# Pairs of batches swept as a wave in a fixed table of issue; value product and keys/values products in eight 64x32 fp32 tiles of TensorE, weights unsplit

## The chip, the cores and the metric

The kernel runs on one core of a Trainium2 chip. The metric is the time that the device takes for one run of the program, in microseconds (us). Lower is better. The kernel before took 899.54, 896.29 and 899.51 us in three runs, a median of 899.51 us. For this kernel, differences under about half a per cent cannot be told from none.

## The reference

An attention over a small memory, then a gated feed-forward block. Batch 8, 8 heads, 576 positions, head size 64, 32 memory slots; 4608 tokens of width 512, and 1536 hidden columns.

```python
a = phi - np.max(phi, axis=2, keepdims=True)
a = np.exp(a)
a = a / (np.sum(a, axis=2, keepdims=True) + 1e-09)
k_m = np.einsum('bhsm,bhsd->bhmd', a, k)
v_m = np.einsum('bhsm,bhsd->bhmd', a, v)
scores = scale * np.matmul(q, k_m.transpose(0, 1, 3, 2))
scores = scores - np.max(scores, axis=-1, keepdims=True)
attn = np.exp(scores)
attn = attn / (np.sum(attn, axis=-1, keepdims=True) + 1e-09)
x = (attn @ v_m), heads side by side      # 4608 x 512
xn = x / np.sqrt(np.mean(x * x, axis=-1, keepdims=True) + 1e-06) * rms_g
g = xn @ w_gate                           # 512 -> 1536
out = (silu(g) * (xn @ w_val)) @ w_out    # 1536 -> 512
```

All inputs and the output are float32. Products on TensorE are either fp32 (each matmul is then two instructions in the profile, a first and a second pass over the weights) or "fp32r" in three terms: an operand is split into a high part and a rest, and high times high, high times low and low times high are added.

## The kernel before, in words

**Pairs and columns.** The eight batches form four pairs. The attention of a token is a row of 32 numbers per head, so `attn @ (v_m @ W)` replaces `(attn @ v_m) @ W`: for each pair and each block of hidden columns, the **value product** (`vw_steps`, L824) multiplies the pair's memory values by the gate and value weights, and the gate and value products (`gv_steps`, L872) multiply the result by the attention rows. There are 12 blocks of 128 hidden columns and 4 pairs, so 48 steps, numbered i in the names (`vp17`, `hf17`).

**Phase 1.** For every batch: the maximum of phi (`prep`, L485: `mc` L493, `mt`, `mx`, `mb`, `mr`), the subtraction (L526), the exponential (L536), the keys/values product `kvp` (`kv_steps`, L556; matmuls at L567 in 128x64 tiles, in which the exponentials `e_bd` are laid out as two heads with zero blocks between them, and sums at L582), and a transpose of the result. Pairs 0 and 1 are attended here: queries are turned (`qtp`, L679), scores `S` L700, maximum and subtraction L711 and L713, exponential L720, sums and norm L727 to L740, then transposes of the attention rows (`tp`, L189, copied at L199), the product that gives each token's square (`xp` L240, L253), its root by Newton steps (L264 to L281), and the scaling and splitting of the attention rows (`rp` L209, `at` L217, `ath` L228, `atl` L229).

**Sweeps.** Pairs 0 and 1 go through the 12 column blocks first, then pairs 2 and 3. A step i is: the value product, 12 fp32r matmuls of 256 columns (L843), split by ACT and DVE into `xh` (L867) and `xl` (L868); four gate and four value products of 6 matmuls, 256 or 320 columns wide (L890), with silu on ACT (`sg` L898) and the multiplication on DVE (`hf` L899); the split of the hidden rows into `hh` on ACT (L912) and `hl` on POOL (L913). Every second i, the output product `po` (L932): 54 matmuls of 512 columns over two blocks, added into `acc` on ACT (L937) or DVE (L939). Pairs 2 and 3 are attended by `attend_steps` (L959) in the first sweep.

**Weights.** They come as 64-bit numbers; `convert` (L340) makes them float32 with bit operations (abs L349, clamp L350, shift L359, add L366, join L379), and splits all of them into a high and a low part (`wh`, `oh` L396 on ACT; `wl`, `ol` L397 on POOL). The split parts are written to memory and read back for the second sweep (`reload`, L410).

**What sets the order.** Each step is entered into a list with a due time from a table of numbers (`PRM`); the sorted list is the program, and the tool that builds it then orders the instructions by its own estimate. The order is fixed when the program is built. Each engine, and SP's queue of transfers, works through its own list in that order; it waits where an operand or a buffer is not ready.

Of the kernel before, what the change touches and what calls it, by code (L numbers as in the profile page):

```python
# [19 lines left out]
XTTR = True  # L20

# [3 lines left out]
WB = 3  # L25
PRM = dict(
    K_AT=[12.08, 15.05, 41.68, 67.52, 100.72, 122.69, 147.6, 167.28],
    KP=0.82,
    POST=[-0.15, 3.05, 3.9, 7.72, 15.27, 21.96],
    P1=4.13,  # L30
    PREP=[-1.56, 0.79, 2.32, 3.9, 18.7],
    PD=[2.1, 11.67, 7.79, 18.42, 7.54, 2.17],
    EXP=[1.89, 13.89, 3.07, 6.96, 11.93, 1.72],
    ES=1.16,
    PH=[9.86, 15.89, 41.23, 73.43, 103.91, 132.92],
    S_AT=[32.67, 47.44, 51.02, 69.42, 103.56, 112.2, 119.41, 123.39],
# [12 lines left out]
    CV2=155.67,
    CP2=0.05,  # L50
    QE=[0, 0],
    CE=[2, 1],
    XE=[28, 29, 14, 13],
    ESN=[3, 3, 2, 3, 3, 3, 2, 3],
    SUM=[1, 0, 1, 0, 2, 1, 2, 1],
    CA=1,
    B=[2, 2, 2],
    RO=3.35,
    RS=4.63,
    RP=2.84,  # L60
    GV=[0.12, 0.256, 0.267, 0.683, 0.84, 0.979],
    VW=[-0.204, 0.03, 0.165],
    VW0=0.296,
    O=[0.115, 0.297, 0.451, 0.524, 0.954, 0.957, 1.344, 1.487, 1.518],
    PRE=[-0.525, 1.142, 1.893, 2.147, 2.545, 2.788],
    PI=0.0157,
    PSW=[1.728, 2.047, 2.009, 2.653, 2.96, 3.24],
    SU=[1.874, 3.014, 5.716, 6.6, 9.746, 12.208, 13.357, 15.533],
    AO=[0.162, 0.169, 0.192, 0.276, 0.385, 0.474, 0.562, 0.581, 0.59, 0.601, 0.728, 0.804, 1.158, 1.217],
    XB=[17.199, 22.916],  # L70
    XS=[0.1086, 0.0359],
    XM=[21.887, 24.858],
    XN=[0.012, 0.176, 0.184, 0.33, 0.33, 0.566, 0.596, 0.699, 0.766],
    LV=[22.571, 24.198],
    CB=1,
)


def weave(*lists):

    order = []
    for li, entry in enumerate(lists):
        steps, lo, hi = entry if isinstance(entry, tuple) else (entry, 0.0, 1.0)
        n = len(steps)
        for i, s in enumerate(steps):
            order.append((lo + (hi - lo) * (i + 0.5) / n, li, i, s))
    order.sort(key=lambda e: e[:3])  # L90
    for e in order:
        e[3]()
# [3 lines left out]
def kernel(  # L96
# [12 lines left out]

    nc = tc.nc
    P = 128
# [9 lines left out]
    G = 2  # L133
# [7 lines left out]
    vm = {}  # L141
    gram = {}
    gb = persist.tile([P, 2, 2, P], F32, name="gb")
    dram = ctx.enter_context(tc.tile_pool(name="dram", bufs=1, space=bass.MemoryType.DRAM))
    gram_dram = {i: dram.tile([P, 2, 2, 64], F32, name=f"gd{i}") for i in range(G, NP)}
    a_dram = {i: dram.tile([P, NT, 256], F32, name=f"ad{i}") for i in range(G, NP)}
    rinv = [persist.tile([P, NT], F32, name=f"rinv{i}") for i in range(NP)]
    at_hi, at_lo = {}, {}

    vg_dram = {b: dram.tile([P, HP, 64], F32, name=f"vgd{b}") for b in range(2 * G, B)}  # L150
    km_late = {b: persist.tile([P, HP, 64], F32, name=f"km{b}") for b in range(2 * G, B)}
    ssqs = {}
    w_dram = {j: dram.tile([P, 2, HP, 2, P], F32, name=f"wd{j}") for j in range(NJ)}
    o_dram = {j: dram.tile([P, 2, 512], F32, name=f"od{j}") for j in range(NJ)}

    def new_vm(pr):
        vm[pr] = persist.tile([P, 2, 2, 2, 2, 64], F32R, tag=f"vm{pr % G}", name=f"vm{pr}")

    def split_v(b, vg):
        pr, j = divmod(b, 2)  # L160
        for e in range(2):
            o = e ^ j
            src = vg.rearrange("p (c e) m -> p c e m", e=2)[:, :, o, :]
            hi, lo = vm[pr][:, 0, :, e, o, :], vm[pr][:, 1, :, e, o, :]
            nc.scalar.copy(hi, src)
            nc.gpsimd.tensor_tensor(out=lo, in0=src, in1=hi.bitcast(F32), op=ALU.subtract)

    def x_steps(pr, a, psum_t, psum_x, fetch=None):

        tps, xps, srcs, st = {}, {}, {}, {}  # L170
        i = pr % G

        def first():
            st["at"] = persist.tile([P, NT, 2, P], F32, tag="at", name=f"at{pr}")
            ssqs[pr] = persist.tile([P, NT], F32, tag=f"ssq{i}", name=f"ssq{pr}")
            for par in range(2):
                rows = slice(64 * par, 64 * par + 64)
                (nc.scalar.copy if pr < G else nc.sync.dma_start)(gb[rows, :, :, rows], gram[pr][rows])

        def turn(t0):  # L180
            n = min(2, NT - t0)

            def f():
                tps[t0] = tp = psum_t(f"tp{pr}_{t0}")
                for t in range(t0, t0 + n):
                    srcs[t] = src = a(t)
                    for cc in (1, 0):
                        o = 2 * (t - t0) + cc
                        nc.tensor.transpose(  # L189
                            out=tp[:, o * P:(o + 1) * P], in_=src[:, cc * P:(cc + 1) * P],  # L190
                            identity=ident,
                        )
            return f

        def copy(t0):
            n = min(2, NT - t0)

            def f():
                (nc.scalar.copy if PRM["XE"][pr] & (1 << t0 // 2) else nc.vector.tensor_copy)(  # L199
                    st["at"][:, t0:t0 + n].rearrange("p t c x -> p (t c x)"), tps.pop(t0)[:, :256 * n]  # L200
                )
            return f

        def spread(t0, n):

            def f():
                tps["r", t0] = tp = psum_t(f"rp{pr}_{t0}")
# [6 lines left out]
            def g():  # L214
                at = st["at"][:, t0:t0 + n]
                tp = tps.pop(("r", t0))[:, :n * P].rearrange("p (t x) -> p t x", x=P)
                nc.vector.tensor_tensor(  # L217
# [902 lines left out]
```

## Time and profile before

| | before |
|---|---|
| runs | 899.54, 896.29, 899.51 us (median 899.51) |
| the profiled execution's own time | 896.89 us |
| its span in the trace | 895.1 us |
| PE busy | 835.6 us (93%), 6207 matmul instructions |
| DVE busy | 559.0 us (62%) |
| ACT busy | 422.0 us (47%) |
| POOL busy | 286.7 us (32%) |

The profile divides the span by engine and by source line. A matmul's duration in it is its passage through a pipeline, longer than the distance to the next one: what a stream of matmuls costs is read from the start times. In the names, the number of the buffer is left out; the arrow points from inputs to output.

### The profile page before, as it was taken

The numbers are of one execution on the slowest core, as the hardware profiler recorded it, in microseconds if no ns is written. First come the engines' busy times: TensorE is split into PE (matmuls) and PEld (weight loads), VectorE is DVE, ScalarE is ACT, GpSimd is POOL, SyncE is SP. The second block draws the span as 40 slices with busy tenths as digits, with TensorE's granted clock in tenths as the row PEclk, the third lists the DMA queues.
The fourth block names the chain that finished last, engine by engine and source line by source line (L and its number), as shares of the span: only waits on it lengthen the run. The fifth ranks groups of instructions, "written<-read, shape, count | busy, mean of one in ns | idle before, by whom it ended". The sixth has DMA issues, their size and how long they took to land.

```text
span 895.1 us, 15791 instructions
## 1 busy us (share of the span) xinstructions
PE 835.6 (93%) x6207; PEld 741.3 (83%) x6207; DVE 559.0 (62%) x956; ACT 422.0 (47%) x719; POOL 286.7 (32%) x242
## 2 busy tenths in 40 slices
PE   4989586999998999999999999899999999999997
PEld 4777476899987988897788997898889999999996
DVE  5577958985778868878845746622545555455543
ACT  2666435787765645656532532344333323333330
POOL 3463735533524414323422421511211112211120
PEclk9899788999999999999999999999999999999999
DMA  8987553652644422534222143502204012040046
GB/s 292 320 263 239 204 169 101 223 168 60 217 114 153 150 61 95 163 105 142 102 73 93 60 117 102 135 1 72 70 4 139 1 63 79 1 142 1 9 110 141
DMA packets 81506, 106.41 MB, mean 119 GB/s; under 512 B 34324, under 2 KB 52248, under 8 KB 81432
## 3 DMA queue, kind: packets, MB, share of 16 engines
q1 hardware_dynamic: 81432, 105.41, 38.0%
q8 instruction: 49, 0.80, 0.4%
q14 instruction: 25, 0.20, 0.1%
HBM read 73.93 MB, written 31.46 MB: 118 GB/s over the span
## 4 chain that ended last, share of the span: by engine, by line
PE 74%; DVE 10%; issue 5%; DMA 5%; ACT 4%; POOL 1%; SPq 1%; DVEq 0%; POOLq 0%; ACTq 0%
PE po L932 29%; PE pv L890 15%; PE pg L890 14%; PE vp L843 6%; PE kvp L567 3%; DMA phi<-in_phi_dram 2%; PE xp L240 2%; DVE w L379 2%; DVE xl L868 1%; DVE ex L350 1%; DMA raw<-in_moe_w_out_dram 1%; PE qtp L679 1%; PE S L700 1%; DVE acc L939 1%; DVE mc L493 1%
## 5 line engine op out<-in xcount | busy, mean ns | idle before, releaser
L913 POOL TENSOR_TENSOR hl<-hf,hh 128x512 fp32r<-128x512 f32 (+1 forms) x96 | 141.4, 1474 | 405.9 <-ACT hh L912 392.3
L939 DVE TENSOR_TENSOR acc<-po,acc 128x512 f32<-128x512 f32 x180 | 123.1, 687 | 128.2 <-PE po L932 127.6
L932 PE MATMUL po<-oh,hh 128*128 128x512 f32 x432 | 172.4, 400 | 3.0 <-DVE acc L939 2.0
L932 PE MATMUL po<-oh,hl 128*128 128x512 f32 x432 | 170.6, 395 | 0.0
L932 PE MATMUL po<-ol,hh 128*128 128x512 f32 x432 | 170.4, 394 | 0.0
L898 ACT ACTIVATE sg<-pg 128x256 f32<-128x256 f32 x192 | 78.1, 411 | 163.2 <-PE pg L890 151.6
L868 DVE TENSOR_TENSOR xl<-vp,xh 64x1024 fp32r<-64x1024 f32 x94 | 114.7, 1220 | 52.3 <-ACT xh L867 51.2
L899 DVE TENSOR_TENSOR hf<-pv,sg 128x256 f32<-128x256 f32 x192 | 85.2, 452 | 71.6 <-PE pv L890 49.0
L867 ACT CAST xh<-vp 64x1024 fp32r<-64x1024 f32 x94 | 94.8, 1008 | 49.7 <-PE vp L843 23.9
L912 ACT CAST hh<-hf 128x512 fp32r<-128x512 f32 (+1 forms) x96 | 64.7, 674 | 81.9 <-DVE hf L899 59.5
L932 PEld LDWEIGHTS po<-oh,hl 128*128 128x128 f32 x432 | 81.2, 188 | 19.3
L932 PEld LDWEIGHTS po<-oh,hh 128*128 128x128 f32 x432 | 81.1, 188 | 17.0 <-DVE acc L939 2.9
L890 PE MATMUL pg<-ath,xh 128*128 128x320 f32 (+1 forms) x384 | 87.3, 300 | 5.7 <-ACT sg L898 3.0
L932 PEld LDWEIGHTS po<-ol,hh 128*128 128x128 f32 x432 | 81.3, 188 | 11.0
L843 PE MATMUL vp<-wh,vm 128*128 128x256 f32 x384 | 85.4, 286 | 3.6 <-DVE xl L868 2.8
L890 PE MATMUL pv<-ath,xh 128*128 128x320 f32 (+1 forms) x384 | 85.0, 299 | 1.1 <-DVE hf L899 0.9
L890 PE MATMUL pg<-atl,xh 128*128 128x320 f32 (+1 forms) x384 | 84.9, 297 | 0.0
L890 PE MATMUL pg<-ath,xl 128*128 128x320 f32 (+1 forms) x384 | 84.7, 295 | 0.0
L890 PE MATMUL pv<-atl,xh 128*128 128x320 f32 (+1 forms) x384 | 84.5, 296 | 0.0
L890 PE MATMUL pv<-ath,xl 128*128 128x320 f32 (+1 forms) x384 | 83.2, 296 | 0.0
L890 PEld LDWEIGHTS pg<-ath,xh 128*128 128x128 f32 x384 | 63.5, 189 | 12.0 <-ACT sg L898 4.8
L843 PEld LDWEIGHTS vp<-wh,vm 128*128 128x128 f32 x384 | 65.4, 189 | 6.7 <-DVE xl L868 2.3
(129 smaller groups left out, 1338.3 us busy)
## 6 DMA issues: line engine op xcount, KB each, us to landing
kv<-in_k_dram SPq DMA_DIRECT2D x32, 288.0 KB, 5.2
kv<-in_v_dram SPq DMA_DIRECT2D x32, 288.0 KB, 5.8
out_dram<-acc SPq DMA_DIRECT2D x72, 128.0 KB, 2.4
raw<-in_moe_w_gate_dram SPq DMA_DIRECT2D x12, 512.0 KB, 5.0
raw<-in_moe_w_val_dram SPq DMA_DIRECT2D x12, 512.0 KB, 3.9
wd<-wh SPq DMA_DIRECT2D x12, 512.0 KB, 3.4
wd<-wl SPq DMA_DIRECT2D x12, 512.0 KB, 4.2
raw<-in_moe_w_out_dram SPq DMA_DIRECT2D x12, 512.0 KB, 4.2
```

Of the source, the lines that this page charges most:

```text
L240: nc.tensor.matmul(xp[64 * j:64 * j + 64, P * cc:P * cc + P], st["at"][:, t, cc, 64 * j:64 * j + 64], gb[:, j, cc], start=True, stop=True,)
L567: nc.tensor.matmul(kvp[64 * par:64 * par + 64, cc, 0:128], e_bd[j][:, hp, c, :], st["kv", b, hp][:, :, 64 * c:64 * c + 64], start=(c == 0) ...
L843: nc.tensor.matmul(vp[:, e, :], lhs(l), r[:, 2 * cc + e, :], start=(n == 0), stop=(n == 2),)
L867: nc.scalar.copy(xh[rows], src)
L868: nc.vector.tensor_tensor(out=xl[rows], in0=src, in1=xh[rows].bitcast(F32), op=ALU.subtract)
L890: nc.tensor.matmul(pt[:, :N], l[:, cc, b, half * P:half * P + P], r[:, b, cc, t0:t0 + n, :].rearrange("p t x -> p (t x)"), start=(m == 0), ...
L898: nc.scalar.activation(sg[:, :N], pg[:, :N], AF.Silu)
L899: nc.vector.tensor_tensor(out=hf[:, :, b, :], in0=pv[:, :N].rearrange("p (t x) -> p t x", x=64), in1=sg[:, :N].rearrange("p (t x) -> p t x ...
L912: nc.scalar.copy(hh, hv)
L913: nc.gpsimd.tensor_tensor(out=hl, in0=hv, in1=hh.bitcast(F32), op=ALU.subtract)
L932: nc.tensor.matmul(po, l[:, tt, :], r, start=(m == 0), stop=(m == 5))
L939: nc.vector.tensor_tensor(out=accs[key], in0=po, in1=accs[key], op=ALU.add)
```

## The change

1. **Wave.** The two sweeps become one list of 24 pairs of blocks, `ORDER`, in which pair 0 starts alone, pair 1 joins after four double blocks, and pairs 2 and 3 follow one after the other. Only pair 0 is attended ahead of the sweep; the products of batches 2 to 7 and the attention of pairs 1 to 3 are issued among the sweep's steps.
2. **Table of issue.** All steps are cut into single instructions or small groups (2933 in all), and a table `ISSUE` gives the place of each; `perform` issues them in that order, and the builder's own ordering is switched off.
3. **Value product.** 16 fp32 matmuls of 64 rows by 32 columns of weights and 256 moving columns (L1002) in place of 12 fp32r matmuls of 128x128. The gate and value weights stay unsplit (`wc`), and so do the memory values (`vm`); what is stored and read back halves. `xh` and `xl` are made in two instructions of 128x512 (L1020, L1018) in place of two of 64x1024.
4. **Keys/values product.** 64x32 tiles without the zero blocks, 72 matmuls per batch (L436) in place of 36 in 128x64 tiles.
5. **Smaller edits.** The weights' last step (join) goes from DVE to POOL (L948); Newton's steps go from four to three, and the root is done in two parts (`fin`); the sums of the attention rows are all on DVE.

```diff
@@ (value product)
-                for e in range(2):
-                    def lhs(vt):
-                        return vt[:, cc, e].rearrange("p o x -> p (o x)")
-                    for n, (l, r) in enumerate(((vh, wh), (vh, wl), (vl, wh))):
-                        nc.tensor.matmul(
-                            vp[:, e, :], lhs(l), r[:, 2 * cc + e, :],
-                            start=(n == 0), stop=(n == 2),
-                        )
+            for cc in range(2):
+                for b in range(2):
+                    for g in range(4):
+                        hp, h = 2 * cc + g // 2, g % 2 ^ flip(b, cc)
+                        rows = slice(64 * h, 64 * h + 64)
+                        nc.tensor.matmul(
+                            vp[32 * g:32 * g + 32, flip(b, cc), cc, :],
+                            vm[pr][rows, b, hp, 32 * (g % 2):32 * (g % 2) + 32],
+                            w[rows, hp, :],
+                            start=True, stop=True,
+                        )
@@ (keys/values product)
+                for c in range(c0, c1):
+                    for cc, hp, rows, to in tiles():
+                        nc.tensor.matmul(
+                            st["kvp", b][cc][to, 0:128],
+                            e_of(b)[rows, hp, c, :],
+                            st["kv", b, hp][rows, :, 64 * c:64 * c + 64],
+                            start=(c == 0), stop=(c == NT - 1),
+                        )
@@ (order of the blocks)
+ORDER = [
+    (0, 0), (0, 1), (0, 2), (0, 3), (1, 0), (0, 4), (1, 1), (0, 5), (1, 2), (1, 3), (1, 4), (1, 5), (2, 0), (2, 1), (2, 2), (2, 3), (2, 4), (2, 5), (3, 0), (3, 1), (3, 2), (3, 3), (3, 4), (3, 5),
+]
```

`flip(b, cc)` is `(b + cc) % 2`. For one half of the batch (cc, b) the four matmuls use both row halves and all four column groups, and all four write the same bank of PSUM; each b takes the row halves the other way round, so the two b together name all eight tiles.

**Where instructions stand now.** On PE late in the sweep. Before, `vp33` is the value product of step 33, `wh17` and `wl17` its split weights, `pv31` and `pg31` a value and a gate product of step 31, `po29` an output product:

```order
L932 MATMUL po29_5_7238<-ol15_7108,hh29_1_7093 128x512
L932 MATMUL po29_5_7238<-oh15_7107,hl29_1_7094 128x512
L890 MATMUL pv31_10_7331<-ath3_6446,xh31_7137 128x320 x2
L890 MATMUL pv31_10_7331<-atl3_6447,xh31_7137 128x320 x2
L890 MATMUL pv31_10_7331<-ath3_6446,xl31_7138 128x320 x2
L843 MATMUL vp33_7347<-wh17_7246,vm2_5874 128x256
L843 MATMUL vp33_7347<-wl17_7247,vm2_5874 128x256
L843 MATMUL vp33_7347<-wh17_7246,vm2_5874 128x256 x2
L843 MATMUL vp33_7347<-wl17_7247,vm2_5874 128x256
L843 MATMUL vp33_7347<-wh17_7246,vm2_5874 128x256
L890 MATMUL pg31_11_7354<-ath3_6446,xh31_7137 128x320 x2
L890 MATMUL pg31_11_7354<-atl3_6447,xh31_7137 128x320 x2
```

After, at the corresponding kind of place (`vp40` is the value product of step 40, `wc40` its unsplit weights):

```order
L1095 MATMUL po37_0_8870<-oh37_8694,hh37_0_8713 128x512
L1095 MATMUL po37_0_8870<-ol37_8695,hh37_0_8713 128x512
L1095 MATMUL po37_0_8870<-oh37_8694,hl37_0_8715 128x512
L1002 MATMUL vp40_8879<-wc40_7763,vm3_6254 32x256 x16
L1095 MATMUL po37_2_8901<-oh36_8835,hh36_0_8603 128x512
L1095 MATMUL po37_2_8901<-ol36_8836,hh36_0_8603 128x512
L1095 MATMUL po37_2_8901<-oh36_8835,hl36_0_8606 128x512
```

All sixteen stand together, between two groups of 128x128 matmuls. Before, the rows show six of the twelve, of the same tile size as their neighbours; the other six stand further on.

On PE before the first gate product, the products of all eight batches, here the last one, stood ahead of it (`kvp7`, and `rp1`, the second pair's scaling):

```order
L582 MATMUL kvp7_1617<-ones_118,es7_1546 64x1 x2
L582 MATMUL kvp7_1617<-ones_118,e_bd1_132 64x1
L582 MATMUL kvp7_1617<-ones_118,es7_1546 64x1 x2
L582 MATMUL kvp7_1617<-ones_118,e_bd1_132 64x1
L209 MATMUL rp1_0_1752<-ident_58,rinv1_71 128x128 x4
L209 MATMUL rp1_4_1762<-ident_58,rinv1_71 128x128 x4
L611 MATMUL kvt7_1747<-ident_58,kb7_1743 128x128 x2
L611 MATMUL kvt7_1747<-ident_58,vb7_1744 128x128 x2
L209 MATMUL rp1_8_1768<-ident_58,rinv1_71 128x128
L636 MATMUL kvt7_1747<-vt7_1758 64x64 x4
L843 MATMUL vp0_0_1804<-wh0_1361,vm0_456 128x256
```

After (`vp2`, the third value product; `mr3`, the maximum of the fourth batch; `pv0` and `pg0`, value and gate products; `kvp3`, the fourth batch's keys/values product):

```order
L1002 MATMUL vp2_1141<-wc2_1002,vm0_469 32x256 x16
L378 MATMUL mr3_0_1165<-ident_72,mb3_0_1058 128x128
L1038 MATMUL pv0_10_1170<-ath0_1103,xh0_847 128x320 x2
L1038 MATMUL pv0_10_1170<-atl0_1108,xh0_847 128x320 x2
L1038 MATMUL pv0_10_1170<-ath0_1103,xl0_882 128x320 x2
L1038 MATMUL pg0_00_1188<-ath0_1103,xh0_847 128x256 x2
L1038 MATMUL pg0_00_1188<-atl0_1108,xh0_847 128x256 x2
L1038 MATMUL pg0_00_1188<-ath0_1103,xl0_882 128x256 x2
L1038 MATMUL pv0_00_1195<-ath0_1103,xh0_847 128x256 x2
L1038 MATMUL pv0_00_1195<-atl0_1108,xh0_847 128x256 x2
L1038 MATMUL pv0_00_1195<-ath0_1103,xl0_882 128x256 x2
L436 MATMUL kvp3_0_1208<-kv3_0_1011,e_bd1_126 32x128 x2
```

Batches 3 to 7 have moved behind the first gate and value products.

On DVE around the first multiplication of gate and value (`hf0`): weights (`ex2`, `w2`) and the split of the value products (`xl0`, `xl1`) stood ahead of it, and all of phase 1 before them:

```order
L858 TENSOR_TENSOR xl0_1819<-vp0_0_1804,xh0_1818 64x512 x2
L858 TENSOR_TENSOR xl0_1819<-vp0_1_1811,xh0_1818 64x512 x2
L350 TENSOR_SCALAR ex2_1_1967<-ex2_1_1967 128x512
L359 TENSOR_SCALAR ex2_1_1967<-ex2_1_1967 128x512
L366 SCALAR_TENSOR_TENSOR ex2_1_1967<-raw_21_1733,ex2_1_1967 128x512
L379 ISA w2_1_1982<-mi2_1_1970,ex2_1_1967 128x1024
L868 TENSOR_TENSOR xl1_1892<-vp1_1839,xh1_1891 64x1024
L899 TENSOR_TENSOR hf0_0_1846<-pv0_00_1848,sg0_00_1861 128x4x64
```

After (`at0` is the first pair's scaling, `wex` the weights, `phi3` the fourth batch's subtraction):

```order
L1018 TENSOR_TENSOR xl1_1117<-vp1_1039,xh1_1060 128x512
L767 TENSOR_TENSOR at0_679<-at0_679,rp0_8_1126 128x256
L934 SCALAR_TENSOR_TENSOR wex1_3_1086<-raw_13_1005,wex1_3_1086 128x512
L387 TENSOR_TENSOR phi3_754<-phi3_754,mr3_0_1165 128x1152
L915 TENSOR_SCALAR wex2_1_1182<-wex2_1_1182 128x512
L927 TENSOR_SCALAR wex2_1_1182<-wex2_1_1182 128x512
L934 SCALAR_TENSOR_TENSOR wex2_1_1182<-raw_21_1084,wex2_1_1182 128x512
L1054 TENSOR_TENSOR hf0_0_1205<-pv0_00_1195,sg0_00_1203 128x4x64
L1054 TENSOR_TENSOR hf0_1_1244<-pv0_10_1170,sg0_10_1241 128x5x64
```

What comes ahead of the first `hf` is now one pair's attention, batches 0 to 2 and the start of batch 3; batches 3 to 7 and three pairs' attention follow it.

More of the change, by code (lines that the diff above doesn't have):

```diff
@@ L95, with flat, perform @@
+ON_SCALAR = (21, 28, 14, 13)
+ISSUE = [
[159 rows of a table added]
+]
+def flat(f):
+    return [h for g in f for h in flat(g)] if isinstance(f, list) else [f]
+def perform(tc, parts):
+    assert sorted(ISSUE) == list(range(len(parts)))
+    with tc.manual_schedule():
+        for n in ISSUE:
+            parts[n]()
 @with_exitstack
@@ L168, in x_steps @@
[L168 to L176, printed above, removed]
+    at_hi, at_lo, vm, gram, ssqs = {}, {}, {}, {}, {}
+    ones = sl.tile([P, 1], F32, name="ones")
+    V.memset(ones, 1.0)
+    hmask = sl.tile([P, 3], F32, name="hmask")
@@ new lines, with flip, bank @@
+    for g in range(4):
+        for c in range(3):
+            V.memset(hmask[32 * g:32 * g + 32, c:c + 1], float((g + c) % 2 == 0))
+    rg = sl.tile([P, HP], F32, name="rg")
+    def flip(b, cc):
+        return (b + cc) % 2
+    e_bd = {}
+    e_bd[0] = persist.tile([P, 2, HP, NT, M], F32, tag="ath1", name="e_bd0")
+    e_bd[1] = persist.tile([P, 2, HP, NT, M], F32, tag="atl1", name="e_bd1")
+    nc.gpsimd.memset(gb, 0.0)
+    def bank(tag, name, shape=None):
+        return ps.tile(shape or [P, 512], F32, tag=tag, name=name)
@@ new lines, with load_rg, put_rg, small @@
+    for t in ("vw",):
+        ps.tile([P, 2, 2, 256], F32, tag="vw", name="vw_first", bufs=1)
+    for t in "gvo":
+        bank(t, f"{t}_first")
+    load = nc.sync.dma_start
+    st = {}
+    def load_rg():
+        rows = st["rg_rows"]
+        st["rg_ps"] = tp = bank("o", "rg_ps")
+        nc.tensor.transpose(out=tp[:, :HP], in_=rows, identity=ident[:HP, :HP])
+    def put_rg():
+        V.tensor_copy(rg, st["rg_ps"][:, :HP])
+    def small(b):
+        return sa if b < 2 else sl
+    def load_phi(b):
+        if b < 2:
+            t = sa.tile([P, HP, NT, M], F32, tag="phi", name=f"phi{b}")
+        else:
+            t = sl.tile([P, HP, NT, M], F32, tag="phi", name=f"phi{b}")
+        n = 2 if b == 0 else HP
+        for i in range(0, HP, n):
+            load(
+                t[:, i:i + n].rearrange("p hp c m -> p hp (c m)"),
+                phi[b].rearrange("(hp h) (p c) m -> (h p) hp (c m)", h=2, c=NT)[:, i:i + n],
+            )
+        st["phi", b] = t
@@ new lines, in f, with add @@
+            return [mm, add] + ([put] if u == NU - 1 else [])
+        return [f(t) for t in range(NT)]
+    parts = []
+    def add(*steps):
+        parts.extend(flat(list(steps)))
+    load_phi(0)
+    st["rg_rows"] = sa.tile([HP, P], F32, name="rg_rows", bufs=1)
+    load(st["rg_rows"], rms_g.rearrange("(hp r) -> hp r", r=P))
+    for hp in range(HP):
+        load_kv(0, hp)
+    load_phi(1)
+    for hp in range(HP):
+        load_kv(1, hp)
+    add(prep(0, 0, 2), prep(0, 2, 4)[:-1], prep(1))
@@ L1080 @@
-    for a, p in enumerate(PRM["SU"]):
-        ev += place(p, PRM["AO"], attend_steps(G + a // HP, a % HP))
-    for a in range(NP - G):
-        steps = x2(G + a)
-        n = len(steps) - 9
-        ev += [(PRM["XB"][a] + PRM["XS"][a] * x, f) for x, f in enumerate(steps[:n])]
-        ev += place(PRM["XM"][a], PRM["XN"], steps[n:])
-        ev.append((PRM["LV"][a], lambda a=a: late_vm(G + a)))
-    for _, f in sorted(ev, key=lambda e: e[0]):
-        f()
+            add(out_steps(i))
+    perform(tc, parts)
```

1318 lines of the change are left out of this document (569 added, 749 removed), and 159 rows, old and new, of the table ISSUE.

## The prediction

> **What bounds the kernel now.** I read the busy shares first, then the table by stage, then the chain of waits, the start times of matmuls, and the groups by line.
>
> ```profile
> span 895.1 us, 15791 instructions
> ...
> PE 835.6 (93%) x6207; PEld 741.3 (83%) x6207; DVE 559.0 (62%) x956; ACT 422.0 (47%) x719; POOL 286.7 (32%) x242
> ```
>
> PE is busy 93% of the span, but not evenly. The table by stage (from:to, length, then busy time of PE, PEld, DVE, ACT, POOL, the granted clock, the DMA share, GB/s) divides the span at the first and the last multiplication of gate and value:
>
> ```profile
> 0.00:50.00 50.00, 36.39 (x454) 30.70 (x456) 29.39 (x58) 23.21 (x38) 21.43 (x27) 0.90 0.89 301
> 50.00:100.00 50.00, 42.56 (x659) 35.39 (x655) 39.07 (x85) 31.38 (x55) 28.77 (x34) 0.97 0.70 233
> 100.00:156.00 56.00, 38.79 (x414) 33.68 (x414) 40.99 (x92) 23.10 (x45) 28.03 (x28) 0.79 0.49 155
> 156.00:250.00 94.00, 91.34 (x644) 83.45 (x645) 74.23 (x112) 74.48 (x131) 40.25 (x27) 1.00 0.56 172
> 250.00:430.00 180.00, 170.71 (x1205) 150.61 (x1203) 139.01 (x219) 102.68 (x166) 58.91 (x42) 1.00 0.40 124
> 430.00:600.00 170.00, 166.34 (x1090) 146.08 (x1091) 97.46 (x191) 68.12 (x123) 51.72 (x46) 1.00 0.29 82
> 600.00:875.00 275.00, 274.60 (x1686) 249.68 (x1685) 130.90 (x193) 97.82 (x162) 56.05 (x39) 1.00 0.18 57
> 875.00:895.10 20.10, 14.85 (x66) 11.76 (x64) 7.96 (x12) 1.17 (x2) 1.57 (x1) 0.97 0.66 153
> ```
>
> ```profile
> L899 DVE TENSOR_TENSOR hf<-pv,sg x192: 402/426/493, 158.3 to 876.0; 128x256 f32<-128x256 f32 x96, 128x320 f32<-128x320 f32 x96
> ...
> 875.84 14.02 PE po L932 x60
> ```
>
> (The second line is from the chain of waits: start, length, what.) For 156 us phase 1 runs, and no engine is full: PE 117.7 us of 156, DVE 109.5 (70%). From 158.3 us the sweep runs, and PE is its bound: 97, 95, 98 and at last 99.9% busy. So the kernel can become shorter in two ways: the sweep starts earlier, or PE has less to do in it.
>
> **PE's prices, from start times.** A matmul's listed duration is its passage; the distance to the next start is its price.
>
> ```profile
> 743.19 0.40 PE L932 MATMUL po<-oh,hh 128*128 128x512 f32 x1
> 743.42 0.40 PE L932 MATMUL po<-ol,hh 128*128 128x512 f32 x1
> ...
> 745.06 0.45 PE L890 MATMUL pg<-ath,xh 128*128 128x320 f32 x2
> 745.35 0.45 PE L890 MATMUL pg<-atl,xh 128*128 128x320 f32 x2
> ...
> 747.99 0.28 PE L843 MATMUL vp<-wh,vm 128*128 128x256 f32 x1
> 748.10 0.28 PE L843 MATMUL vp<-wl,vm 128*128 128x256 f32 x1
> 748.22 0.40 PE L843 MATMUL vp<-wh,vm 128*128 128x256 f32 x2
> 748.46 0.29 PE L843 MATMUL vp<-wl,vm 128*128 128x256 f32 x1
> ```
>
> 512 columns cost 0.2325 us (mean of a run of them), 320 columns 0.147 (0.29 for two), 256 columns 0.118 (0.47 for the four from 747.99 to 748.46). One step i before: value product 12 x 0.118 = 1.42; gate and value 24 x 0.147 + 24 x 0.118 = 6.35; output product 27 x 0.2325 = 6.28; together 14.05. The 60 output matmuls of the end (14.02) agree: 60 x 0.2325 = 13.95. The change leaves gate, value and output products as they are: 48 x 12.63 = 606 us that stay.
>
> **Value product in 64x32 tiles.** The trace has no 64x32 tile and no row halves; the nearest rows are phase 1's 128x64 tiles in fp32.
>
> ```profile
> 38.80 1.26 PE L567 MATMUL kvp<-kv,e_bd 128*64 128x128 f32 x20
> 39.99 0.33 PE L517 MATMUL mr<-ident,mb 128*128 128x128 f32 x1
> 40.25 1.30 PE L700 MATMUL S<-km,qT 128*64 128x64 f32 x36
> 41.49 0.66 PE L679 MATMUL qtp<-ident,qr 128*128 128x128 f32 x4
> 42.07 1.52 PE L567 MATMUL kvp<-kv,e_bd 128*64 128x128 f32 x22
> 43.53 0.66 PE L679 MATMUL qtp<-ident,qr 128*128 128x128 f32 x4
> ```
>
> 22 instructions of `kvp` take 1.46 us up to the next form and 20 take 1.19. If about 0.1 of each is the change of tile size, one instruction is 0.055 to 0.06 us, for 128 columns. The two 64-column halves work side by side, so each instruction holds its half for 0.109 us; 256 columns hold a tile for 0.218. S (64 columns, 36 in 1.24 less the change) gives 0.031 each, the same scale. Each fp32 matmul is two instructions: the 36 matmuls of a batch are 72 of the profile. The 16 of the new value product are 32 instructions of 0.218.
>
> - all eight tiles at once: 32 / 8 x 0.218 = 0.87 us;
> - four at once: 1.74 us;
> - two at once, which is all that the trace shows: 32 / 2 x 0.218 = 3.49 us.
>
> Two changes of tile size per product come on top, 0.19 us by the rows above. So the price lies between 1.06 and 3.68 us against 1.42 before: from 0.36 less to 2.26 more, per step. I take 1.06. The eight tiles are eight different row-and-column parts of the array, and the halves that the rows show side by side are likewise parts of it. Feeding them is no bound: S starts an instruction every 0.031 us, and 32 x 0.031 is 1.0.
>
> Here a page of the Trainium skill speaks against the change. "TensorEngine Tiling (Array Packing)", section "Restrictions and Gotchas", says that different row tiles cannot access the same PSUM bank simultaneously. In the new order the four matmuls of a batch half use both row halves and write one bank. Taken by the letter, only half of the tiles work at a time, the case of four above. "PSUM — Partial Sum Buffer" (key terms) divides a bank further into quadrants of 32 partitions, and here each column group writes its own, which speaks for eight. No trace here settles it.
>
> **The keys/values product** is 288 matmuls, 576 instructions of 0.0545, 31.4 us in all; the new one is 576 matmuls, 1152 instructions of 0.109 / 8, 15.7 us. Squares, scores and transposes stay. With the small products by the same prices (about 69 us) and 182 changes of tile size at 0.094 (17 us), PE's sum after is 606 + 42 + 16 + 69 + 17 = **750 us**.
>
> **When the sweep starts.** DVE had 111 us of work ahead of the first `hf` (109.5 by the stages, up to 156 us). The new order puts less there:
>
> ```profile
> L366 DVE SCALAR_TENSOR_TENSOR ex<-raw,ex 128x512 int32<-128x512 int32 x36 | 33.7, 937 | 0.6
> L350 DVE TENSOR_SCALAR ex<-ex 128x512 f32<-128x512 f32 x36 | 23.4, 651 | 10.9 <-ACT ex L349 10.6
> L359 DVE TENSOR_SCALAR ex<-ex 128x512 int32<-128x512 int32 x36 | 21.9, 607 | 0.6
> L493 DVE TENSOR_REDUCE mc<-phi 128x128 f32<-128x1152 f32 x7 | 15.1, 2159 | 4.7 <-DMA phi<-in_phi_dram 4.6
> L526 DVE TENSOR_TENSOR phi<-phi,mr 128x1152 f32<-128x1152 f32 x7 | 9.5, 1352 | 14.6 <-PE mr L517 14.6
> L713 DVE TENSOR_TENSOR ex<-S,mxs 128x576 f32<-128x576 f32 x8 | 6.0, 752 | 0.2
> L858 DVE TENSOR_TENSOR xl<-vp,xh 64x512 fp32r<-64x512 f32 x4 | 2.7, 687 | 0.1
> L939 DVE TENSOR_TENSOR acc<-po,acc 128x512 f32<-128x512 f32 x180 | 123.1, 687 | 128.2 <-PE po L932 127.6
> L898 ACT ACT_TABLE_LOAD x9 | 11.5, 1283 | 0.2
> ```
>
> Ten weight tiles at 0.651 + 0.607 + 0.937 = 22.0 us; four batches' maxima 8.7 (three of 2.16, two halves of 1.1) and subtractions 5.6 (half the work for the first); four score chains of 2.8 (11.2: two operations at 0.75, the sums, small ones); squares 5.1; root and Newton 7.8; the scaling of keys and values 7.2; four `xl` at 0.687 2.7; copies and scaling of attention rows 4.2; small ones 4.2: **79 us**, 32 less. PE has 37 us there, ACT 48. If DVE is busy as in phase 1 before (70%), the first `hf` comes at 112 us; if always, at 79. I take 83%, 95 us: the loads ahead are fewer (two batches' keys and values, not eight, in a stage where the DMA share was 0.89), and the weights fill waits.
>
> The rest of phase 1 isn't gone. Between the first `hf` and those of step 9 stand another 141 us on DVE: 22 weight tiles (49), `hf` (18), 26 output additions at 0.687 (18), `xl` (14), the other pairs' chains (42). PE's own work ahead of step 9's gate product is only 170 us in all. So **DVE bounds the first ten steps**; they end at 95 + 141 / 0.95 = 243 us. From there PE has 750 - 170 = 580 us left, DVE 525 - 220 = 305, ACT 244 and POOL 153 by the same count: PE bounds. I add 12 us for PE's waits (3% until the last pair is attended, about 300 us, as from 156 to 600 before; 1% after) and 3 for the last additions and stores: 243 + 580 + 12 + 3 = 838 us of span. The profiled run was 1.8 us above its span (896.89 and 895.1): **840 us**. The median of the runs before is 899.51, 2.6 above the profiled run's own time, so I do not correct further.
>
> What costs nothing: the join on POOL (busy 287 of 895 us before, 274 by the new count); 34 table loads on ACT instead of 18 (16 x 1.28 = 21 us, beside ACT's idle half); the sums moved to DVE and the third Newton step dropped are in the 79 and the 141. The halved weight store and reload is off the path once the sweep runs (DMA share 0.40 and less from 250 us). In the first ten steps ACT has 155 us of work in 243, table loads included; were it late there, the 21 us would be the price. The fixed order adds waits by position: behind a held `hf` on DVE stand the weight tiles, for which the POOL join and so the next value product wait. That is the price in rival 3.
>
> **Rivals.**
>
> 1. *Four tiles at once.* Then 0.87 us more per step, 38 steps behind the DVE-bound stage: 33 us, **873**. For it: the page above, and that the trace shows two abreast and no more. Against: each column group has its own 32 partitions.
> 2. *Two at once, slower than before.* Then 2.62 more per step, 38 x 2.62 = 100 us: **940**. The mechanism is that rows and columns of tiles do not overlap beyond two, as in the only rows that there are; the product then takes 3.68 us of PE against 1.42. It decides as soon as the value product costs over 840 + 38 x extra = 897, extra 1.5, that is 2.56 us, fewer than three tiles abreast on average. Against: nothing in the rows says that two is the limit; 128x64 has no more than two tiles.
> 3. *The fixed table is ill-timed, or the front is not shortened.* First `hf` at 112 us, and DVE 80% busy after it, as from 156 to 250 before (74.2 of 94): 112 + 141 / 0.8 = 288, then 595: **885**. For it: DVE was 70% busy in phase 1 and waited for PE and transfers. Against: the order before was fixed at build time, too, and waits there were for `kvp` and phi, which now cost half or come later.
> 4. *Everything fits.* First `hf` at 85, DVE full: 85 + 141 + 580 + 8 = 814, and **800** if the DVE operations are also a tenth shorter than their means.
>
> **How the numbers follow.** Forecast 840 (805 to 862): 0.62. Four abreast (860 to 885): 0.13. Ill-timed front (860 to 893): 0.11. Two abreast (905 to 960): 0.09. Under 805: 0.05. The range of 8 in 10 is 802 to 880: it holds the forecast and most of cases 1 and 3. Half a per cent is about what a measurement of this kernel can tell from no change. Faster by over 0.5% (below 895): 0.62 + 0.13 + 0.10 + 0.05 = 0.90, less 0.02 for mishaps in the front: 0.88. Within: 0.03. Slower: 0.09, nearly all case 2.
>
> **What would show it.** Right: 32 instructions of the value product within 1.1 us including both changes of tile size; first `hf` near 95 us; DVE over 90% busy from there to 240; PE over 97% behind 250 and 99% behind 450; period of four steps 4 x 13.7 = 55 us late in the sweep, against 56.2. Wrong: a value product of 1.9 us (four abreast) or 3.7 (two); first `hf` behind 110; DVE idle before `hf` for gate or value in the first ten steps; a last step that ends well behind PE's last matmul.

## The result, and the profile after

The changed kernel takes 832.05 us (median of four runs, 830.76 to 833.51) against 898.28 before (896.29 to 899.54, four runs): a ratio of 0.9265, with a 95% interval of 0.9236 to 0.9294. The forecast was 840, with a range of 802 to 880. The profiled execution took 833.51 us, its span is 831.7.

The first lines of the page of the kernel after: span, and busy time, share and instructions of each engine.

```profile
span 831.7 us, 19077 instructions
...
PE 788.9 (95%) x7903; PEld 672.6 (81%) x7903; DVE 459.2 (55%) x1014; ACT 364.0 (44%) x683; POOL 264.7 (32%) x223
```

PE has 1696 more matmul instructions and 46.7 us less busy time. Outside its busy time it had 59.5 us (895.1 - 835.6) and has 42.8 (831.7 - 788.9). Of the 63.4 us that the span lost, **46.7 are busy time of PE and 16.7 its idle time**. Busy time counts passages, so it is not yet a price: by start times (further on), the keys/values product accounts for about 19 of the 46.7 and the value product for 9; the rest was not taken apart. The table by stage of the kernel after, in the columns of before, divided at the first multiplication of gate and value:

```profile
0.00:85.80 85.80, 55.23 (x1123) 42.22 (x1124) 59.15 (x170) 41.97 (x75) 34.53 (x41) 0.84 0.76 259
85.80:150.00 64.20, 62.42 (x654) 54.36 (x660) 46.56 (x97) 50.49 (x95) 34.03 (x27) 1.00 0.70 201
150.00:250.00 100.00, 98.75 (x1231) 84.57 (x1216) 81.52 (x180) 57.61 (x102) 53.37 (x44) 1.00 0.65 212
250.00:430.00 180.00, 180.00 (x1489) 155.73 (x1488) 96.61 (x211) 79.36 (x148) 53.02 (x43) 1.00 0.42 130
430.00:600.00 170.00, 168.58 (x1777) 144.68 (x1776) 84.96 (x202) 70.20 (x131) 40.07 (x33) 1.00 0.42 123
600.00:800.00 200.00, 199.72 (x1520) 170.77 (x1519) 80.03 (x143) 59.73 (x125) 43.94 (x33) 1.00 0.26 80
800.00:831.70 31.70, 24.22 (x129) 20.26 (x127) 10.39 (x18) 4.62 (x9) 5.71 (x4) 0.95 0.43 109
```

```profile
L1054 DVE TENSOR_TENSOR hf<-pv,sg x192: 409/427/493, 85.8 to 816.8; 128x256 f32<-128x256 f32 x96, 128x320 f32<-128x320 f32 x96
```

The sweep starts at 85.8 us instead of 158.3. From there PE is 97% busy at once, and DVE 73% (46.56 of 64.20): PE is the bound from the first gate product on. Who made PE wait between 86 and 231 us (the first ten steps) is a short list (total us, times, longest):

```profile
PE po L1095 <- DVE acc L1104: 0.9, 1, 0.9
PE qtp L647 <- ACT qT L653: 0.9, 1, 0.9
PE qtp L647 <- DVE acc L1104: 0.8, 1, 0.8
PE rp L759 <- DVE acc L1104: 0.3, 1, 0.3
```

That is 2.9 us in 145. DVE, in turn, waits ahead of `hf` in the same stretch, 5.1 and 5.8 us, most of it for PE (busy us, mean ns, then idle before and what ended it):

```profile
L1054 DVE TENSOR_TENSOR hf<-pv,sg 128x320 f32<-128x320 f32 x19 | 9.1, 485 | 5.1 <-PE pv L1038 3.7 <-ACT sg L1049 1.4
L1054 DVE TENSOR_TENSOR hf<-pv,sg 128x256 f32<-128x256 f32 x20 | 8.3, 418 | 5.8 <-PE pv L1038 4.4 <-ACT sg L1049 1.4
```

The start times of a value product late in the kernel after (start, us, engine, line, operation, count):

```profile
783.76 0.46 PE L1038 MATMUL pg<-ath,xl 128*128 128x320 f32 x2
784.15 1.09 PE L1002 MATMUL vp<-wc,vm 64*32 64x256 f32 x32
785.17 0.56 PE L1038 MATMUL pg<-ath,xh 128*128 128x320 f32 x2
785.57 0.45 PE L1038 MATMUL pg<-atl,xh 128*128 128x320 f32 x2
```

The 32 instructions hold PE from 784.15 to 785.17, 1.02 us. The two 320-column matmuls ahead of them take 0.39 instead of 0.29, and the two behind them 0.40: 1.23 us with both changes of tile size, against 1.42 before, 0.19 less in each of 48 steps (9 us). In the single records, eight instructions start 7 ns apart, the next eight 0.24 us after the first, the third and fourth groups 0.216 us apart. Eight tiles work at once. (The program gives the sixteen matmuls of a product to the same four tiles in its first and last quarter, and to the other four between them.)

### The profile page after: what moved, and what is told of

It reads as the page before. It is cut to its first block, busy times and chain, and to the rows that moved or that the text cites. A ratio compares the mean times of both kernels' runs of the same rounds, so it can differ in the third digit from the quotient of the medians.

```text
span 831.7 us, 19077 instructions
## 1 busy us (share of the span) xinstructions
PE 788.9 (95%) x7903; PEld 672.6 (81%) x7903; DVE 459.2 (55%) x1014; ACT 364.0 (44%) x683; POOL 264.7 (32%) x223
## 3 DMA queue, kind: packets, MB, share of 16 engines
q8 instruction: 62, 1.02, 0.5%
## 4 chain that ended last, share of the span: by engine, by line
PE 84%; DVE 6%; ACT 3%; DMA 3%; issue 2%; SPq 1%; POOLq 0%; POOL 0%; DVEq 0%; ACTq 0%
PE po L1095 34%; PE pg L1038 18%; PE pv L1038 17%; PE vp L1002 6%; PE kvp L436 2%; PE xp L794 2%; PE S L665 2%; DMA raw<-in_moe_w_val_dram 1%; PE qtp L647 1%; DMA kv<-in_v_dram 1%; PE tp L739 1%; DVE xl L1018 1%; DVE wex L915 1%; DVE wex L934 1%; DVE mc L350 1%
## 5 line engine op out<-in xcount | busy, mean ns | idle before, releaser
L1069 POOL TENSOR_TENSOR hl<-hf,hh 128x512 fp32r<-128x512 f32 (+1 forms) x96 | 137.9, 1440 | 381.3 <-ACT hh L1064 365.2
L1049 ACT ACTIVATE sg<-pg 128x256 f32<-128x256 f32 (+1 forms) x192 | 77.3, 412 | 182.4 <-PE pg L1038 148.4
L1054 DVE TENSOR_TENSOR hf<-pv,sg 128x256 f32<-128x256 f32 (+1 forms) x192 | 85.0, 453 | 127.2 <-PE pv L1038 71.7
L1095 PEld LDWEIGHTS po<-oh,hh 128*128 128x128 f32 x432 | 81.3, 188 | 22.6 <-issue 3.5
L1038 PE MATMUL pg<-ath,xh 128*128 128x256 f32 (+1 forms) x384 | 87.6, 309 | 0.1
L1038 PE MATMUL pg<-ath,xl 128*128 128x256 f32 (+1 forms) x384 | 82.3, 296 | 0.0
L1020 ACT CAST xh<-vp 128x512 fp32r<-128x512 f32 x96 | 54.5, 587 | 62.5 <-PE vp L1002 30.3
L1038 PE MATMUL pg<-atl,xh 128*128 128x256 f32 (+1 forms) x384 | 81.8, 294 | 0.0
L1018 DVE TENSOR_TENSOR xl<-vp,xh 128x512 fp32r<-128x512 f32 x96 | 64.1, 684 | 30.8 <-ACT xh L1020 30.8
L1038 PEld LDWEIGHTS pv<-ath,xh 128*128 128x128 f32 x384 | 64.1, 190 | 9.4 <-issue 2.3
L1038 PEld LDWEIGHTS pv<-atl,xh 128*128 128x128 f32 x384 | 61.8, 189 | 0.0
```

The source lines that it names most:

```text
L1018: V.tensor_tensor(out=xl[:, k], in0=src, in1=xh[:, k].bitcast(F32), op=ALU.subtract)
L1020: nc.scalar.copy(xs[i][0][:, k], src)
L1038: nc.tensor.matmul(pt[:, :N], l[:, flip(b, cc), cc, half * P:half * P + P], r[:, b, cc, t0:t0 + n, :].rearrange("p t x -> p (t x)"), start ...
L1049: nc.scalar.activation(sg[:, :N], acts[gi, b, 0][:, :N], AF.Silu)
L1054: V.tensor_tensor(out=acts[gi][:, :, b, :], in0=acts[gi, b, 1][:, :N].rearrange("p (t x) -> p t x", x=64), in1=acts[gi, b, 2][:, :N].rearr ...
L1069: nc.gpsimd.tensor_tensor(out=hl, in0=acts[gi].rearrange("p t b x -> p t (b x)"), in1=hsplit[i, gi][0].bitcast(F32), op=ALU.subtract,)
```

## The experiments

Two theories stood after the result. **P**: PE bounds from the first gate product on, and PE time counts one to one. **D**, the prediction's: DVE bounds the first ten steps, to about 243 us, and PE behind them. A third question was whether the gain sits in the operations or in the table that orders them. Medians are of four runs each; the kernel before, run with them on the same chips, took 899.43 (a1, b1, c1, d1), 900.12 (a2, c2, e1, f1) and 900.66 us (e2, j1, m12). The changed kernel itself was not run again beside them, so a difference of about 4 us (half a per cent) or less from its 832.05 is taken as real only where a trace shows where it comes from. The columns of all profile rows are as above.

**a1_four_tiles: the order within the value product.**

```diff
-            for cc in range(2):
-                for b in range(2):
-                    for g in range(4):
+            for cc, b in ((0, 0), (1, 1), (0, 1), (1, 0)):
+                    for g in sorted(range(4), key=lambda g: g % 2):
```

> Same 16 matmuls per value product, in another order: the two batch halves that use the same four tiles stand together, so only four tiles have work at a time. Theory P (PE bounds from the first gate product on): 0.87 us more in each of 48 steps, 832 + 42 = 874 us. Theory D (of the prediction: DVE bounds the first ten steps): 38 x 0.87 = 33 more, 865 us. If a later tile's matmul can pass an earlier one that waits for its tile, no change, 832 us. In the profile, the 32 instructions then take 1.6 us from first to last start, against 0.72.

835.3 us (831.97 to 836.47), ratio 0.9279 (0.9238 to 0.932). The value product at the same place of this kernel:

```profile
785.57 1.12 PE L1001 MATMUL vp<-wc,vm 64*32 64x256 f32 x32
786.62 0.56 PE L1037 MATMUL pg<-ath,xh 128*128 128x320 f32 x2
```

1.05 us instead of 1.02: not 0.87 more but 0.03. Eight instructions still start together, now in two fours 53 ns apart. The third outcome of the expectation holds: an instruction whose tile is free does not stay behind one that waits for its tile, at least over these sixteen. (The signal that ends a product fits this: by start time it stands on the 28th of the 32 records in the changed kernel, whose last matmul in the program uses the four tiles that start first in each round, and on the 32nd here, where the last one uses those that start second.) This did not test the price of four tiles; that needed the next one.

**a2_same_four_tiles: only four tiles are used.**

```diff
-                        hp, h = 2 * cc + g // 2, g % 2 ^ flip(b, cc)
+                        hp, h = 2 * cc + g // 2, g % 2
```

> All sixteen matmuls of a value product go through the same four of the eight tiles (each b takes the row halves the same way round, so heads are mixed up and the output is not the reference's). Same count, same sizes. Theory P (PE bounds from the first gate product on): 32 instructions on four tiles are 8 x 0.216 = 1.73 us in place of 0.86, so 48 x 0.86 = 41 more, 873 us. Were P right only after the first ten steps: 865. If the order of a1 cost nothing because four tiles already suffice (the tiles are not what limits), 832.

870.23 us (867.88 to 871.63), ratio 0.9682 (0.9638 to 0.9726): 38 more than the changed kernel. Its value product:

```profile
798.96 1.93 PE L1002 MATMUL vp<-wc,vm 64*32 64x256 f32 x32
800.82 0.50 PE L1095 MATMUL po<-oh,hh 128*128 128x512 f32 x1
```

1.86 us instead of 1.02, 0.84 more; 48 x 0.84 is 40. This is rival 1's price, close to its 873, and the case did not occur. The 38 lie between P (41) and D (33), and do not decide between them.

**b1_vp_twice_first10, c1_xl_twice_first10, c2_no_xl_first10: which engine bounds the first ten steps.**

```diff
@@ b1, in the value product
+            for cc, b in [(cc, b) for _ in range(2 if i < 10 else 1) for cc in range(2) for b in range(2)]:
@@ c1, in the evacuation
+                    for _ in range(2 if i < 10 else 1):
                         V.tensor_tensor(out=xl[:, k], in0=src, in1=xh[:, k].bitcast(F32), op=ALU.subtract)
@@ c2, in the evacuation
+                if low and i < 10:
+                    return
@@
+                if k == 0 and low and i < 10:
+                    xs[i].append(xs[i][0])
```

> The value product is issued twice in the first ten steps only, the second writing the same values. P: 10 x 0.87 = 9 us more, 841 us. D: DVE hides it, 832 to 834 us.

> The subtraction that makes xl is issued twice on DVE in the first ten steps only (20 x 0.684 = 13.7 us more of DVE work). P: under 3 us more, 832 to 835 us. D: 13.7 more, 846 us.

> In the first ten steps xl is not made, and xh stands in its place in the products (the low part is left out there); DVE has 13.7 us less, PE the same. P: PE waits for 3 us in all between 86 and 231 us, so at most 3 us less there and 2 before the first gate product, 828 to 832. D (DVE bounds the first ten steps): 10 or more less, 818 to 822. After c1 (8.6 more for 13.7 of DVE work) I expect the two to be unequal: adding DVE work hurts, taking it away helps little, if both engines are nearly full there.

b1: 843.11 us (842.06 to 844.87), ratio 0.938 (0.9347 to 0.9413), 11 more for 9 us of PE work; 5 of them come ahead of the first `hf` (91.0 us), where three of the ten products stand (twice the 2.6 us that they were expected to cost; why stays open), and 6 behind it for the other seven, one to one. c1: 840.62 (838.63 to 841.83), ratio 0.9348 (0.9314 to 0.9383), 8.6 more for 13.7 of DVE work. c2: 829.25 (828.82 to 829.99), ratio 0.9229 (0.9191 to 0.9268), 2.8 less. PE work in the first ten steps counts in full, so D falls. Taking 13.7 us from DVE gives 2.8, of which 1.6 come ahead of the first `hf` (84.2 us), where D expected 10 or more; PE is then full behind it, as the row of c2 shows:

```profile
85.80:150.00 64.20, 64.17 (x717) 56.35 (x716) 43.21 (x90) 52.28 (x98) 35.43 (x28) 1.00 0.73 215
```

So DVE is not the bound. But adding 13.7 costs 8.6, which pure P did not expect: DVE has little to spare. Two stages of c1 show where it goes, the one before the sweep and one of the first ten steps:

```profile
0.00:88.00 88.00, 55.77 (x1121) 42.65 (x1122) 61.96 (x174) 42.30 (x75) 34.54 (x41) 0.88 0.74 252
...
150.00:231.00 81.00, 76.55 (x736) 63.89 (x735) 71.62 (x155) 47.62 (x84) 44.16 (x36) 1.00 0.63 200
```

The first `hf` comes at 88.0 us (2.2 later), and PE is idle 4.4 us of the 81 from 150 to 231, where the changed kernel has 1.3 (79.75 busy). Both engines are nearly full there in c1, PE with 76.55 of 81 us and DVE with 71.62.

**j1_join_on_dve: the weights' join back on DVE.**

```diff
-            nc.gpsimd.tensor_tensor(out=w.bitcast(I32), in0=m, in1=ex, op=ALU.add)
+            V.tensor_tensor(out=w.bitcast(I32), in0=m, in1=ex, op=ALU.add)
```

> The weights' join goes back from POOL to DVE (36 instructions of about 1.0 us, 10 of them ahead of the first gate product, 22 in the first ten steps). P in its pure form: the 10 in front count, behind it only what exceeds DVE's 29 us of idle time there, 842. By the half that c1 showed (6 of 11 us behind the first gate product): 832 + 10 + 12 = 854. If the join is hidden on either engine: 832.

846.84 us (844.83 to 851.0), ratio 0.9398 (0.9373 to 0.9424): 14.8 more, between the two outcomes of the expectation (842 and 854). The first `hf` comes at 91.2 us, 5.4 later. The rest comes behind it, where PE waits more:

```profile
150.00:231.00 81.00, 76.54 (x608) 62.73 (x607) 73.39 (x162) 45.70 (x80) 28.16 (x23) 1.00 0.62 197
```

With the table left as it is, the small edit that took this work off DVE is worth more than the new tiles of the value product (14.8 against 9 us). Whether another table would hide the join on DVE was not tried.

**d1_kvp_twice: more of the keys/values product.**

```diff
-                    for cc, hp, rows, to in tiles():
+                    for r, (cc, hp, rows, to) in [(r, x) for r in range(2) for x in tiles()]:
...
-                            start=(c == 0), stop=(c == NT - 1),
+                            start=(c == 0 and r == 0), stop=(c == NT - 1 and r == 1),
@@
-    V.memset(ones, 1.0)
+    V.memset(ones, 2.0)
```

> Every matmul of the keys/values product is issued twice, so that the product is twice as large, and the sum that divides it is made with 2 in place of 1. The extra 1152 instructions are 15.7 us of PE at eight tiles abreast. P: the 12 us of batches 2 to 7 count in full, the 4 of batches 0 and 1 partly, 844 to 849 us. D: what falls into the first ten steps (batches 2 to 4) is hidden, 838 to 841 us. Were two tiles abreast, it would be 63 us more, 890 us.

866.84 us (864.14 to 869.77), ratio 0.9643 (0.9604 to 0.9682): 35 more, where P gave 12 to 17 and D 6 to 9. The first `hf` comes at 100.7 us, 15 later. The chain of waits of d1 near its start, and of the changed kernel behind it:

```profile
12.16 4.36 PE kvp L436 x202
16.52 3.06 issue
...
26.13 3.11 PE kvp L436 x125
29.24 3.37 issue
```

```profile
21.67 4.29 PE kvp L436 x141
25.96 2.61 issue
```

"issue" is time in which PE waits for nothing that the profile shows. Counted over all of PE's records (matmuls, weight loads and those of its sequencer), the gaps of over 0.7 us amid this product begin behind record 449, 961, 2241, 2497, 3265, 6337, 7361, 11201, 12225 and 12481 in d1, and behind 705 and 10177 in the changed kernel (left out are those near the start that the profile puts down to the exponential or to a load). All these counts have the same remainder, 193, when divided by 256. The trace also has a queue of instruction transfers. Its line on the pages of the changed kernel and of d1:

```profile
q8 instruction: 62, 1.02, 0.5%
q8 instruction: 71, 1.16, 0.6%
```

The packets have 16384 bytes each, and there is one for each 256 records of PE, in both kernels; d1's nine more belong to its 2304 more records (1152 matmuls and as many weight loads). In each of the three stops shown above, one packet, of 1.0 to 1.1 us, lands before PE goes on: at 18.07, 31.28 and 26.94 us, 1.3 to 1.6 us ahead of the next matmul. So PE stops there for its own instructions, which come in blocks of 256: small tiles use them up faster than they come. The Trainium skill, "Runtime: NRT & Kernel Launch", section "Instruction fetch mechanics", has such blocks of 256 instructions, and says that the fetch is hidden by the pace at which instructions are issued; here it is not. What sets how late a block is asked for was not tried. These stops, with one of 2.8 us ahead of a value product, add up to 17.7 us in d1 and 3.8 in the changed kernel: 14 more, which with the 15.7 of the product itself make 30 of the 35. So d1 decides nothing between the theories; the price that both gave the extra product was wrong.

**f1_before_8_of_12: less PE work in the kernel before.**

```diff
-                    for n, (l, r) in enumerate(((vh, wh), (vh, wl), (vl, wh))):
+                    for n, (l, r) in enumerate(((vh, wh), (vl, wh))):
...
-                            start=(n == 0), stop=(n == 2),
+                            start=(n == 0), stop=(n == 1),
```

> The kernel before, with the term of high values times low weights left out of the value product (8 matmuls of 256 columns per step in place of 12: 0.47 us of PE less in each of 48 steps, 22.6 in all). If PE work counts one to one in the sweep before, too: 898 - 22 = 876 us. If the sweep there is held by DVE or by loads in the first half, half of it: 885 or more.

871.49 us (870.06 to 872.41), ratio 0.9695 (0.9645 to 0.9744): 27 to 29 less, for 22.6 of PE work. In the kernel before, too, PE work in the sweep counts in full; the few us above it may be the builder's order, which changes with the program.

**e1_builders_order and e2_vp_in_pieces: the table.**

```diff
@@ e1
-    with tc.manual_schedule():
-        for n in ISSUE:
-            parts[n]()
+    for n in ISSUE:
+        parts[n]()
```

> The same steps entered in the same order, but the builder's own ordering is on, as in the kernel before. If the gain is PE work and the wave, little changes: 832 to 848 us. If the table itself carries it, 860 or more.

965.76 us (960.1 to 968.07), ratio 1.0738 (1.0682 to 1.0795): 134 more; with the same operations and without the fixed table, the kernel is slower than before. PE's line of its page:

```profile
PE 865.0 (90%) x7903; PEld 693.9 (72%) x7903; DVE 478.5 (50%) x1014; ACT 372.6 (39%) x685; POOL 267.1 (28%) x223
```

PE is busy 76 us longer with the same 7903 instructions, and idle 101 us (966.3 - 865.0) instead of 43. The first `hf` comes at 106.9 us, 21 later, and the longest of PE's waits is one for weights read back, which the changed kernel does not have:

```profile
PE po L1094 <- DMA oh<-od: 10.4, 6, 3.7
```

The builder's order broke up the value products: the tile size changes 342 times in the records instead of 183, and only 11 of 48 products have their 32 instructions in a row. e2 tests that alone:

```diff
+        between = [x for x in range(at + 1, end) if ISSUE[x] in big][:3]
+        for kk, part in enumerate(pieces[value[n]]):
+            place = at if kk == 0 else between[kk - 1] if kk <= len(between) else end - 0.5
+            parts.append(part)
+            seq.append((place, 1 if kk == 0 else 2 + kk, len(parts) - 1))
```

(`at` and `end` are the places of the product and of its evacuation, `big` the gate, value and output products.)

> The table is kept, but a value product is cut into its four batch halves where gate, value or output products stand between it and its evacuation: 135 pieces in place of 48 (109 of 4 matmuls, 6 of 8, 9 of 12, 11 of 16). A piece of 4 or 8 matmuls lasts 2 x 0.216 us, one of 12 or 16 lasts 4 x 0.216: 67 us in all against 41; 87 more pieces are 174 more changes of tile size at 0.092 = 16 us. P: 832 + 26 + 16 = 874 us. If the loss of e1 came from elsewhere (loads, waits of order), little, 832 to 845.

887.19 us (885.73 to 889.01), ratio 0.9855 (0.9834 to 0.9876): 55 more: five sixths of the gain of 66 are gone. A product of e2 in three pieces, with the first 128x128 matmuls between:

```profile
559.68 0.64 PE L1003 MATMUL vp<-wc,vm 64*32 64x256 f32 x8
560.25 0.56 PE L1041 MATMUL pv<-ath,xh 128*128 128x320 f32 x2
560.65 0.45 PE L1041 MATMUL pv<-atl,xh 128*128 128x320 f32 x2
560.94 0.45 PE L1041 MATMUL pv<-ath,xl 128*128 128x320 f32 x2
561.32 0.64 PE L1003 MATMUL vp<-wc,vm 64*32 64x256 f32 x8
561.89 0.56 PE L1041 MATMUL pg<-ath,xh 128*128 128x320 f32 x2
```

Eight instructions hold PE 0.57 us, more than half of what 32 need in one piece. The expectation had 0.43 and 0.18 of changes for such a piece; the rows show 0.57, 0.09 more on the matmuls ahead of it (0.38 for 0.29) and 0.11 on the pair behind (0.40 for 0.29), 0.77 in all. Counted in the same way, a product of 16 instructions costs 0.79, of 24 1.20 and of 32 1.23 (the median times of such pieces are 0.59, 1.00 and 1.02); over the expectation's 135 pieces that is 54 us more than 48 x 1.23, and 55 were measured. Such breaking-up can so account for most of PE's extra 76 us in e1 (e2's own PE line has 841.1, 52 more); e1's extra idle time, 58 us, is a matter of other waits, which were not taken apart. What the wave and the table would be worth with the old tile sizes, no run shows.

**m12_tail_and_root: two places of the table.** In order: behind part 2899 stand 2902, 2901, 2903, 2904, 2905 (silu, value product, multiplication, high and low part of the last half step), and behind 206 the parts 977 and 979 (clamp and shift of a weight tile).

```diff
+        seq = list(ISSUE)
+        for after, ns in [(2899, [2902, 2901, 2903, 2904, 2905]), (206, [977, 979])]:
+            seq = [n for n in seq if n not in ns]
+            at = seq.index(after) + 1
+            seq[at:at] = ns
-        for n in ISSUE:
+        for n in seq:
```

> Two places of the table are changed. Tail: the last value product of 320 columns, its silu, multiplication and split go ahead of the first four output products of the last step, so that PE does not wait 0.76 and 0.90 us for them: 1.7 us less. Front: two weight operations on DVE (clamp and shift of one tile) go behind the second multiplication of the attention rows, which frees 1.5 us and a wait of 0.7 ahead of the first gate product: up to 2 less. Together 828 to 831 us, against 832; if the front is set by PE's own queue there (vp2 stands ahead of the first value product), only the tail, 830.5.

828.59 us (827.35 to 829.09), ratio 0.9201 (0.9185 to 0.9217): below the changed kernel's runs (830.76 to 833.51) in every run, by 3.5 us, and faster than both kernels. The first `hf` comes at 83.1 us, 2.7 earlier. PE's two waits in the tail of the changed kernel are gone:

```profile
PE po L1095 <- POOL hl L1069: 0.9, 1, 0.9
PE po L1095 <- ACT hh L1064: 0.8, 1, 0.8
```

The two edits were not run apart.

## Why the prediction was right, and where it was not

- **Direction, size and range** held: 832 in 802 to 880, forecast 840. The likeliest case was the one that happened, eight tiles at once.
- **Value product**, 1.06 us forecast with two changes of tile size: 1.23, beyond the 1.1 that the prediction gave as its own sign. The price from the 128x64 rows held (0.218 us per instruction and tile; 0.216 measured); the two changes of tile size were forecast at 0.19 and cost 0.37. In the changed kernel both row halves write one bank of PSUM, each column group its own 32 partitions, at the full rate of eight tiles. The rule of the Trainium skill that the prediction cites from "TensorEngine Tiling (Array Packing)", section "Restrictions and Gotchas", that different row tiles cannot access one PSUM bank simultaneously, would by the prediction's working have given the time of four tiles, which is a2's 870; the trace does not agree with it. Rivals 1 and 2 fall on the same start times. (The trace of before does hold two instructions on half the rows, `mr` at L517; they show nothing of tiles side by side.)
- **Keys/values product**, 15.7 us forecast: in the start times, distances under 0.3 us add up to 21.7 us (40.6 before, for a forecast of 31.4), and two fetch gaps of 2.6 and 1.2 us come on top. Mechanism right, size off on both sides; the saving, 19 us without the gaps, is near the forecast 15.7. That PE stops for instructions was in no term of the sum.
- **"I take 83%, 95 us"** was 10% too late: 85.8. Two errors cancel in part: the 79 us of DVE work measured 59.2 busy (the listed durations add up to 70.3), and DVE's share stayed at 69% (59.15 of 85.80), as in the kernel before, not 83%. The means came from stages in which the instructions were longer: the weights' three steps on DVE took 0.53, 0.53 and 0.78 us against 0.65, 0.61 and 0.94, and small instructions overlap, so that adding their durations counts time twice (two that start 0.07 us apart are listed with 0.15 each).
- **"DVE bounds the first ten steps"** is the step that failed. From 85.8 us to the end of step 9's products at 231 PE is busy 142.6 us of 145.6 and DVE 116.7 (80%, where the prediction expected over 90%), and b1 and c2 give the bound to PE. The prediction's own sign against this step is there, too: DVE waits 10.9 us for gate and value products ahead of its `hf` between 86 and 231 us (shown above). The forecast had 141 us of DVE work there, and PE's 170 - 37 = 133 beside it: DVE's was over-counted (its listed durations add up to 129.5, its busy time to 116.7) and PE's under-counted, and 148 forecast for the stretch came near the 145 measured by chance. c1 and j1 show how near the other case was: in c1, 14 us more of DVE work cost 9.
- **The rest**, 595 us forecast from there, took 601. Behind the end of PE's last matmul come 5.8 us (5.3 in the kernel before; forecast 3), and 1.7 us of waits for the last split stand ahead of it, which m12 removes.
- **The fixed table (rival 3).** The table was not ill-timed: the first `hf` came at 85.8 us, not at 112. That the order before was just as fixed was used against this rival, and is true, but e1 and e2 show that the point was a different one: with its products broken up by the order, the new tile size costs PE more (52 us of busy time in e2) than it saves (9), and without any table the kernel takes 966 us. The forecast of 840 rested on sixteen matmuls standing together in the rows of the order, which it used for the changes of tile size and did not weigh as a condition.

## What to carry to other kernels

Small tiles of TensorE pay when all of them have work at the same time and the tile size seldom changes: here 32 instructions in a row cost 1.2 us, the same in pieces of eight about 0.8 us each, and most of the gain is lost. Where one engine bounds and a second is nearly full, take away and add the same work on each: only the pair of experiments (2.8 less, 8.6 more) told which of them bound. A sum of listed durations can exceed an engine's busy time (70.3 against 59.2 us on DVE here); check the sum against the busy time of a stage before calling that engine the bound.

## What the runs showed of the hardware that was not expected

- Two row halves of TensorE write one PSUM bank, each column group in its own 32 partitions, at the full rate of eight tiles: 32 instructions of 256 columns in 1.02 us.
- The order of instructions within such a group hardly matters (a1: 0.03 us).
- A group of 64x32 instructions between 128x128 matmuls costs 0.3 to 0.4 us beyond the time of its tiles (1.23 against 4 x 0.216 for 32 instructions, 0.77 against 2 x 0.216 for eight).
- PE stops for 0.8 to 3.4 us at distances of 256 instructions where small tiles use them quickly, and longest near the start; in the three stops shown, a transfer of 16384 bytes of instructions lands 1.3 to 1.6 us before PE goes on.
